# Attention and two MoE layers on one core: a head's cast in two halves, zeros moved to the start of GpSimd, a unit's input copied on chip

## The chip, the cores and the metric

One Trainium2 chip, one of its cores. The metric is the device time of one execution in microseconds (us), as a median of several runs. The engines are TensorE (PE in the profile, with PEld for its weight loads), VectorE (DVE), ScalarE (ACT), GpSimd (POOL) and SyncE (SP, which here only issues DMAs).

## What is computed

The input is `q`, `k`, `v` of 4 batches with 8 heads of 576 rows and 64 columns, a decay factor `f`, and the weights of two feed-forward layers. Everything is float32.

```python
scores = scale * q @ k.T
cum = cumsum(log(clip(f, 0.0001, 1.0)))
scores = where(causal, -1e9, scores + cum[:, None] - cum[None, :])
attn = exp(scores - max(scores)); attn = attn / (sum(attn) + 1e-09)
x = (attn @ v)                    # to 2304 tokens x 512
x = square(max(x @ w_in, 0)) @ w_out          # 512 -> 2048 -> 512
x = elu(x @ w2_in) @ w2_out                   # 512 -> 2048 -> 512
```

## The kernel before, in words

**Precision.** A float32 product is made of three fp32r products of rounded operands: high by high, low by high, high by low. So each operand is first cast to its rounded value and then subtracted from the original for the low part. The cast is `copy` (L125; its VectorE form is L131), the subtraction is `minus` (L119), which on GpSimd is L136.

**Order of the work.** Attention runs in steps, written out in the list `todo`; a head pair has five of them: parts A of both heads, a joint part "4", parts B of both. In each step `soft` (L635) makes the scores and the exponentials, and `outs` (L645) one step later (`LAG`) turns and splits them and multiplies by `v`. Between the pieces, `fill` (L890) puts matmuls of the first feed-forward layer for the first six units of 256 tokens (`unit`, L723). A scheduler with a time line then sets the order in which each engine's queue stands, and the few `tc.issue_after(...)` in the code bind it.

**Scores and row maxima.** A tile of scores is written by TensorE (`scores`, L436; for a rounded head two matmuls per block, L442 and L443), read by VectorE (`reduce_min`, L446, which leaves the negated row maximum in `nm` by an accumulator read), and turned into exponentials by ScalarE (`expo`, L448). The scores have two buffers: the third tile can begin only when VectorE has reduced the first. That is the place where TensorE can wait for VectorE ("s L442 <- DVE nm L446").

**The heads.** Batch 0 is done in plain F32 ("Plain", no cast). The 24 heads of batches 1 to 3 are "rounded" heads of part "F". `load_head` (L398) prepares one, two steps ahead (`AHEAD`): the raw tile of 128x1280 (704 columns for q, 576 for k) is cast to `qk1` by **one VectorE instruction** (L131), four rows of decay go by DMA to `qk2` (L424), GpSimd makes q's low part (64x704, L136), a DMA moves k's rounded part from `qk1` to `qk2` (L427), GpSimd makes k's low part (64x576, L136) and splits v (L129 and L136). `qk1`, `raw` and `qk2` have three buffers each.

**Outputs.** `out_a`, `out_b` and `fold` (L522) gather a head pair's x in 64x256 or 64x320 pieces on VectorE, `split_pt` (L508, lines L509 and L510) splits a turned tile, `norm_x` (L535) scales with one over the row sums, and `store_x` (L547) splits x into `xs` (ScalarE high, L553; low by L123 or L136) and stores it to `x1` in DRAM (L556). `load_x1` (L697) loads a unit's input back as `xu` (L701). The input of unit 0 stays on chip as `x0`.

**Opening.** `block_zeros` (L264) clears, behind a copy named `quiet`, two strips of the tiles of part "4" (`e4s`), a mask `m4` and half an identity, all on GpSimd; it first waits for the cumulated decay.

Of the kernel before, what the change touches and what calls it, by code (L numbers as in the profile page):

```python
# [19 lines left out]
NC = DM // 128  # L20
# [15 lines left out]
PACE = (1.28, 0.9, 1.85, 1.75)  # L36
COST = {'A': 0.7, '4': 1.1, 'B': 1.7}
W_AT = (1, 1, 1, 1, 0, 0, 0, 0, 2, 2, 2, 2, 2, 2)
AHEAD = 2
FETCH = 4  # L40
LAG = 1
# [42 lines left out]
def attention_then_moe_kernel(ctx, tc, first, firstv, plain, qkv, f, w1, w2, out):  # L84
# [125 lines left out]

    fr = ab.tile([32, S], F32, tag="eb", name="fr", bufs=BUFS["eb"])
    nc.sync.dma_start(out=fr, in_=f)
    x0 = xa.tile([128, 2 * NC, CH], F32R, tag="xu", name="x0")
    raws_w = xa.tile([128, 2, 512, 2], I32, tag="xu", name="raws_w")
    mz = a1.tile([128, 512], F32, name="mz")
    m4 = a1.tile([128, 288], F32, name="m4")
    ptA = [[a1.tile([128, 512], F32R, name=f"ptA{s}{t}") for t in range(2)] for s in range(2)]
# [3 lines left out]
    ca = wa.tile([B * H, 4, 512], F32R, tag="w7", name="ca")  # L221
    me.memset(f32(ca[:, 0:2, 256:512]), 1.0)
    me.memset(f32(ca[:, 2:4, 0:256]), 1.0)
    nc.gpsimd.memset(mz, 0.0)
    mask(mz[:, 384:512], [[-1, 128]])

# [37 lines left out]
    def block_zeros():  # L264
        quiet = nc.gpsimd.tensor_copy(go, f32(made[1][:, 1, S - 257:S - 256]))
        with tc.issue_after(quiet.ins):
            for s in range(2):
                nc.gpsimd.memset(e4s[s][:, S:640], 0.0)
            nc.gpsimd.memset(m4, 0.0)
            nc.gpsimd.tensor_copy(ident[:, 128:192], ident[:, 0:64])  # L270
            for k in range(2):
                mask(m4[64 * k:64 * k + 64, 224:288], [[-1, 64]])
# [125 lines left out]
    def load_head(b, h, part):  # L398
        q0, q1, k1, js = {"F": (0, QW, S, 5), "A": (Q0, QW, 256, 2), "B": (0, Q0, S, 5)}[part]
        w = "ABF".index(part)  # L400
        raw = raws.pop((b, h, part))
        if isinstance(raw, Plain):
            return raw
        raw, rv = raw
        vr = rv[:, 0:js * D].rearrange("p (j d) -> p j d", d=D)
        qk1 = hd.tile([128, RAW], F32R, tag="qk1", name="qk1", bufs=BUFS["qs"])
        qk2 = a1.tile([128, RAW], F32R, tag="qk2", name="qk2", bufs=3)
        kc = slice(QW, QW + k1)
        qc = slice(q0, q1)
        g = b * H + h  # L410
        if part == "A":
            ac = slice(Q0, QW + 256)
            copy(ENG["qk"][w], qk1[:, ac], raw[:, ac])
        else:
            ac = slice(0, RAW)
            if part == "F":
                copy(ENG["qk"][w], qk1, raw[:, ac])
            else:
                copy(ENG["qk"][w], qk1[:, qc], raw[:, qc])
                copy(ENG["qk"][w], qk1[:, kc], raw[:, kc])  # L420
        if part == "A":
            nc.sync.dma_start(out=f32(qk2[64:68, ac]), in_=f32(ca[g:g + 1]))
        else:
            nc.sync.dma_start(out=f32(qk2[64:68, ac]), in_=aug[g - H, :, ac])  # L424
        minus(ENG["ql"][w], qk2[0:64, qc], raw[0:64, qc], qk1[0:64, qc])
        if ENG["kh"][w] == "d":
            nc.sync.dma_start(out=f32(qk2[0:64, kc]), in_=f32(qk1[0:64, kc]))  # L427
        else:
            copy(ENG["kh"][w], qk2[0:64, kc], f32(qk1[0:64, kc]))
        minus(ENG["kl"][w], qk1[64:128, kc], raw[64:128, kc], qk1[64:128, kc])  # L430
        vv = hd.tile([128, 5, 2 * D], F32R, tag="vv", name="vv", bufs=BUFS["vv"])
        copy(ENG["vh"][w], vv[:, 0:js, 0:D], vr)
        minus(ENG["vl"][w], vv[:, 0:js, D:2 * D], vr, vv[:, 0:js, 0:D])
        return qk1, qk2, vv
# [112 lines left out]
    def store_x(b, hp, x, c0, n):  # L547
        if b in SPLIT and c0 == 0:
            xs = x0[:, hp::NC]
        else:  # L550
            xs = a1.tile([128, 2, 320], F32R, tag="xs", name="xs", bufs=BUFS["xh"])
        c = slice(0, n)
        nc.scalar.activation(out=xs[:, 0, c], in_=x[:, c], func=AF.Copy)  # L553
        minus(ENG["xl"][b > 0], xs[:, 1, c], x[:, c], xs[:, 0, c])
        if not (b in SPLIT and c0 == 0):
            nc.sync.dma_start(out=x1[b][hp::NC, :, c0:c0 + n].rearrange("c p t -> p c t"), in_=f32(xs[:, :, c]))  # L556

    def out_a(hh, e, x, k):
        pt = ps_t.tile([128, 512], F32, tag="t", name="pt")
# [68 lines left out]
    e4 = {}  # L628
    es = {}
    xs = {}  # L630

    def load(b, hp, k, part):
        heads[b, hp, k] = load_head(b, 2 * hp + k, part)

    def soft(b, hp, kind, k):  # L635
        if kind == "A":
# [58 lines left out]
        return gh, gl  # L695

    def load_x1(t0, n, pool):  # L697
        x = pool.tile([128, 2 * NC, n], F32R, tag="xu", name="xu")
        for c in range(NC):
            for off, step, b, s in runs(t0, n):  # L700
                nc.sync.dma_start(out=f32(x[:, c::NC, off:off + step]), in_=x1[b][c::NC, :, s:s + step].rearrange("c p t -> p c t"))  # L701
        return x
# [145 lines left out]
        return False  # L848

    credit = 0.0  # L850
    for i in range(len(todo) + LAG):
        at_step[0] = i
        if i == 0:
# [11 lines left out]
                aug_rows(True)  # L865
        while fetches and fetches[0][0] <= i + FETCH and i > max(BEGIN):
            fetch_head(*fetches.pop(0)[1:])
        while loads and loads[0][0] <= i + AHEAD:
            load(*loads.pop(0)[1:])
        if i < len(todo):  # L870
            sg = soft(*todo[i])
# [18 lines left out]
        def fill():  # L890
# [14 lines left out]
            if not started[0] and not went and i < FILL_TO:  # L905
                with tc.issue_after(seen[0].ins):
                    busy(FILL + (step == 1))

        drain(sg)
        fill()  # L910
        for _ in og:
            fill()
# [384 lines left out]
```

## Time and profile before

| what | us |
|---|---|
| median of 3 runs | 1026.14 (1025.92 to 1027.38) |
| the profiled execution itself | 1025.79 |
| span in that profile, first to last instruction | 1024.0 |
| PE busy | 1011.2 (99%) |
| DVE busy | 709.2 (69%) |
| ACT busy | 522.9 (51%) |
| POOL busy | 257.3 (25%) |

The first 345 us hold the attention with the first units of the first layer; after that come feed-forward layers alone. The instructions of GpSimd lie almost all in the first 345 us, so that its 25% are more like three quarters there. TensorE's granted clock is 1.00 in nearly all of the span.

### The profile page before, as it was taken

How to read it: one execution, taken by the hardware profiler on the slowest of the kernel's cores; microseconds unless marked ns; L12 is line 12 of the kernel's file. 1: busy time of each engine (PE TensorE's matmuls, PEld its weight loads, DVE VectorE, ACT ScalarE, POOL GpSimd, SP SyncE). 2: the span in 40 equal slices, each digit the busy share in tenths (PEclk: the TensorE clock that was granted, in tenths of full speed). 3: DMA queues.
4: the chain of work that ended last, by engine and by line, in shares of the span. 5: the costliest groups of instructions: out<-in, count | busy, mean ns of one | idle time of the engine just before them, and what ended most of it. 6: DMA issues, size and time to landing. Idle time of an engine off the chain costs nothing.

```text
span 1024.0 us, 17635 instructions
## 1 busy us (share of the span) xinstructions
PE 1011.2 (99%) x6363; PEld 899.2 (88%) x6363; DVE 709.2 (69%) x1595; ACT 522.9 (51%) x1196; POOL 257.3 (25%) x282
## 2 busy tenths in 40 slices
PE   9999999999999999999999999999999999999998
PEld 8777799899999988889988888998889988899997
DVE  8894788766775548845376779895455989654554
ACT  7674676766676634423243445553334555333331
POOL 2135697675774300012104040400000000000000
PEclk9999999999999999999999999999999999999999
DMA  8847547454531074443545645653415556353402
GB/s 212 271 140 208 171 137 227 146 153 124 183 106 62 24 259 125 143 132 116 175 139 211 210 169 197 234 178 113 145 42 185 165 186 207 102 182 126 147 21 83
DMA packets 77334, 157.59 MB, mean 154 GB/s; under 512 B 9616, under 2 KB 38032, under 8 KB 77248
## 3 DMA queue, kind: packets, MB, share of 16 engines
q1 hardware_dynamic: 77232, 156.46, 47.5%
q8 instruction: 50, 0.82, 0.3%
q14 instruction: 36, 0.29, 0.1%
q10 hardware_dynamic: 16, 0.02, 0.0%
HBM read 113.94 MB, written 38.90 MB: 149 GB/s over the span
## 4 chain that ended last, share of the span: by engine, by line
PE 95%; DVE 2%; DMA 1%; ACT 1%; POOL 1%; issue 0%; ACTq 0%; POOLq 0%; SPq 0%
PE O L192 33%; PE P L192 18%; PE pH L192 13%; PE ph L192 7%; PE o L192 6%; PE pt L513 5%; PE pv L520 4%; PE s L438 3%; PE pv L517 2%; PE s L442 2%; PE s L443 2%; PE idle L289 1%; DMA xu<-x 1%; PE pr L513 1%; DVE qk L131 0%
## 5 line engine op out<-in xcount | busy, mean ns | idle before, releaser
L192 PEld LDWEIGHTS P<-xu,v 128*128 128x128 f32 x1536 | 200.1, 189 | 10.8 <-issue 0.5
L192 PE MATMUL P<-xu,v 128*128 128x256 f32 x1536 | 203.7, 282 | 0.7 <-DMA xu<-x 0.7
L192 PE MATMUL O<-v,gh 128*128 128x512 f32 x576 | 171.1, 393 | 0.0
L192 PE MATMUL pH<-xu,w 128*128 128x512 f32 (+1 forms) x672 | 140.8, 360 | 0.0
L192 PEld LDWEIGHTS pH<-xu,w 128*128 128x128 f32 x672 | 114.0, 188 | 20.2
L192 PE MATMUL O<-gh,w 128*128 128x512 f32 (+1 forms) x448 | 122.6, 362 | 0.0
L192 PEld LDWEIGHTS O<-v,gh 128*128 128x128 f32 x576 | 102.8, 188 | 17.6
L1142 ACT ACTIVATE hs<-P 128x256 f32<-128x256 f32 x128 | 48.4, 381 | 113.8 <-PE P L192 113.0
L192 PE MATMUL O<-v,gl 128*128 128x512 f32 x288 | 103.5, 393 | 0.0
L192 PEld LDWEIGHTS O<-gh,w 128*128 128x128 f32 x448 | 79.8, 189 | 14.1
L136 POOL TENSOR_TENSOR yl<-pr,yh 128x512 fp32r<-128x512 f32 x18 | 25.1, 1394 | 248.5 <-ACT yh L962 174.7
L1145 DVE TENSOR_TENSOR hs<-P,hs 128x256 f32<-128x256 f32 x96 | 40.5, 422 | 62.2 <-PE P L192 58.9
L136 POOL TENSOR_TENSOR qk<-raw,qk 64x704 fp32r<-64x704 f32 (+1 forms) x48 | 77.1, 1606 | 17.6 <-DVE qk L131 5.2
L192 PE MATMUL O<-gl,w 128*128 128x512 f32 (+1 forms) x224 | 80.1, 363 | 0.0
L192 PE MATMUL o<-gh,w 128*128 128x256 f32 x384 | 76.1, 292 | 0.0
L157 ACT ACTIVATE wt<-wraw 128x512 f32<-128x512 f32 x57 | 38.4, 673 | 58.5 <-DMA wraw<-in_w_dram 39.4
L192 PE MATMUL ph<-xu,w 128*128 128x256 f32 x480 | 66.8, 287 | 0.3 <-DMA xu<-x 0.3
L682 ACT ACTIVATE gh<-g 128x512 fp32r<-128x512 f32 (+1 forms) x80 | 46.9, 586 | 38.2 <-DVE g L681 34.9
L681 DVE TENSOR_TENSOR g<-g 128x512 f32<-128x512 f32 (+1 forms) x56 | 45.1, 805 | 28.3 <-ACT g L677 28.1
L192 PEld LDWEIGHTS O<-v,gl 128*128 128x128 f32 x288 | 53.1, 188 | 10.3
L1113 ACT ACTIVATE gh<-g 128x512 fp32r<-128x512 f32 x72 | 45.4, 631 | 32.3 <-DVE g L1168 25.4
L192 PEld LDWEIGHTS o<-gh,w 128*128 128x128 f32 x384 | 60.3, 191 | 1.4 <-issue 0.5
(166 smaller groups left out, 2045.5 us busy)
## 6 DMA issues: line engine op xcount, KB each, us to landing
xu<-x SPq DMA_DIRECT2D x66, 512.0 KB
wraw<-in_w_dram SPq DMA_DIRECT2D x57, 512.0 KB
raw<-in_qkv_dram SPq DMA_DIRECT2D x24, 640.0 KB
x<-yh SPq DMA_DIRECT2D x31, 256.0 KB
x<-yl SPq DMA_DIRECT2D x31, 256.0 KB
x<-xs SPq DMA_DIRECT2D x16, 320.0 KB
xu<-x SPq DMA_DIRECT2D x16, 256.0 KB
rv<-in_qkv_dram SPq DMA_DIRECT2D x24, 160.0 KB
```

Of the source, the lines that this page charges most:

```text
L136: nc.gpsimd.tensor_tensor(out=dst, in0=x, in1=f32(hi), op=ALU.subtract)
L157: nc.scalar.activation(out=f32(t), in_=f32(hi), func=AF.Abs)
L192: nc.tensor.matmul(out=dst, lhsT=l, rhs=r, start=first and i == 0, stop=last and i == n - 1, skip_group_check=skip)
L438: seen[0] = nc.tensor.matmul(out=dst, lhsT=hh.t[0:68, hh.q + q0:hh.q + q0 + 128], rhs=hh.t[0:68, hh.k + j0:hh.k + j0 + n], start=first, st ...
L442: nc.tensor.matmul(out=dst, lhsT=qk1[:, q0:q0 + 128], rhs=qk1[:, QW + j0:QW + j0 + n], start=first, stop=False)
L513: seen[0] = nc.tensor.transpose(dst, src, ident[:, c0:c0 + 128])
L520: seen[0] = nc.tensor.matmul(out=dst, lhsT=hh[2][:, J, :], rhs=hl[i], start=first and i == 0, stop=last and i == 1)
L681: (nc.vector if sq == "v" else nc.gpsimd).tensor_tensor(out=g[:, 0:n], in0=g[:, 0:n], in1=g[:, 0:n], op=ALU.mult)
L682: nc.scalar.activation(out=gh[:, 0:n], in_=g[:, 0:n], func=AF.Copy)
L1113: nc.scalar.activation(out=gh, in_=g, func=AF.Copy)
L1142: nc.scalar.activation(out=o, in_=x, func=AF.Copy)
L1145: nc.vector.tensor_tensor(o, y, x, op=ALU.add)
```

## The change

Three edits:

- **Cast in two halves.** `load_head` for a rounded head becomes a generator `whole_head`. Its first half casts q's 704 columns, issues the decay rows and q's low part; it is bound behind the last row maximum of the step in which it is asked for (`reduced[-1]`), and heads are asked for one step earlier (`AHEAD + 1`). In the next step the second half casts k's 576 columns behind the first row maximum of that step, and then issues the DMA of k's rounded part, k's low part and v's split.
- **Zeros.** The two strips of `e4s` are cleared among the first instructions of GpSimd, ahead of the mask `mz`, and no longer in `block_zeros`.
- **Unit 1's input.** Its tile `second` is allocated at step 14 (`OPEN`). When `store_x` has stored the second part of batch 0's x for head pairs 1 to 3, a further DMA copies the first 256 columns from `xs` to that tile on chip, and `load_x1` leaves those three loads out. The store to `x1` stays. The tiles `raws_w` and `x0` of the same pool swap their order of declaration.

```diff
+    for s in range(2):
+        nc.gpsimd.memset(e4s[s][:, S:640], 0.0)
     nc.gpsimd.memset(mz, 0.0)
...
         with tc.issue_after(quiet.ins):
-            for s in range(2):
-                nc.gpsimd.memset(e4s[s][:, S:640], 0.0)
             nc.gpsimd.memset(m4, 0.0)
...
-                copy(ENG["qk"][w], qk1, raw[:, ac])
...
+        with tc.issue_after(behind[0].ins):
+            copy(ENG["qk"][w], qk1[:, qc], raw[:, qc])
...
         minus(ENG["ql"][w], qk2[0:64, qc], raw[0:64, qc], qk1[0:64, qc])
+        yield
+        with tc.issue_after(behind[0].ins):
+            copy(ENG["qk"][w], qk1[:, kc], raw[:, kc])
         if ENG["kh"][w] == "d":
             nc.sync.dma_start(out=f32(qk2[0:64, kc]), in_=f32(qk1[0:64, kc]))
...
             nc.sync.dma_start(out=x1[b][hp::NC, :, c0:c0 + n].rearrange("c p t -> p c t"), in_=f32(xs[:, :, c]))
+            if not b and second:
+                nc.sync.dma_start(out=f32(second[0][:, hp::NC, :]), in_=f32(xs[:, :, 0:CH]))
+                here.add(hp)
...
-        x = pool.tile([128, 2 * NC, n], F32R, tag="xu", name="xu")
+        x = second[0] if t0 == CH else pool.tile([128, 2 * NC, n], F32R, tag="xu", name="xu")
         for c in range(NC):
+            if t0 == CH and c in here:
+                continue
...
-        while loads and loads[0][0] <= i + AHEAD:
+        while loads and loads[0][0] <= i + AHEAD + (loads[0][4] == "F"):
             load(*loads.pop(0)[1:])
...
+        n_red = len(reduced)
         drain(sg)
+        for h in coming:
+            behind[0] = reduced[min(n_red, len(reduced) - 1)]
+            second_half(*h)
+        if i == OPEN:
+            second.append(xa.tile([128, 2 * NC, CH], F32R, tag="xu", name="xu"))
+        coming = halves_[:]
+        halves_.clear()
+        for h in coming:
+            behind[0] = reduced[-1]
+            first_half(*h)
         fill()
```

How the order moves is seen on VectorE in the fourth head pair of batch 1. `ISA eb.., nm..` is a row maximum (its second row reads the accumulator), CAST the cast of a head, `p`, `ptB` the split of a turned tile, `xs`, `xB`, `xA` pieces of the output. Before:

```order
L446 ISA eb_2736,nm2_2737<-s_2739,mz_126 128x512
L446 ISA nm2_2737 128x1
L131 CAST qk1_2762<-raw_2663 128x1280
L446 ISA eb_2736,nm2_2737<-s_2744,mz_126 128x384
L446 ISA nm2_2737 128x1
L510 TENSOR_TENSOR ptB01_133<-pt_2513,ptB00_132 128x256
L123 TENSOR_TENSOR xs_2418<-xA_2344,xs_2418 128x256
L510 TENSOR_TENSOR p1_2557<-pt_2552,p0_2556 128x320
L446 ISA eb_2772,nm2_2773<-s_2774,mz_126 128x512
L446 ISA nm2_2773 128x1
```

Now (the line numbers have moved by two):

```order
L448 ISA eb_2741,nm2_2742<-s_2744,mz_126 128x512
L448 ISA nm2_2742 128x1
L132 CAST qk1_2697<-raw_2631 128x576
L454 TENSOR_SCALAR z1_2678<-z1_2678 128x1
L448 ISA eb_2741,nm2_2742<-s_2749,mz_126 128x384
L448 ISA nm2_2742 128x1
L132 CAST qk1_2760<-raw_2673 128x704
L512 TENSOR_TENSOR p1_2567<-pt_2562,p0_2566 128x320
L512 TENSOR_TENSOR p1_2575<-pt_2570,p0_2574 128x320
L531 TENSOR_TENSOR xB_2493<-pv_2510,t_2547 64x320
L448 ISA eb_2778,nm2_2779<-s_2780,mz_126 128x512
L448 ISA nm2_2779 128x1
```

Between the row maxima of 512 and 384 columns, which free the two score buffers, a whole cast of one head stood; now the k half of one head stands there, and a q half of another behind the second row maximum.

The second place is SP's queue at the end of batch 0, where the last pieces of unit 1's input are issued (`x1_0` and `x1_1` are batch 0 and 1 in DRAM; `xu_1469` and `xu_1041` are the tile of unit 1, `xu_2717` and `xu_2732` that of the unit after it). Before:

```order
L556 DMA x1_0_71<-xs_1435 128x2x320
L427 DMA qk2_1830<-qk1_1829 64x576
L306 DMA rv_2034<-in_qkv_dram 128x320
L701 DMA xu_1469<-x1_0_71 128x2x256
L701 DMA xu_2717<-x1_0_71 128x2x64
```

Now:

```order
L558 DMA x1_0_71<-xs_1440 128x2x320
L560 DMA xu_1041<-xs_1440 128x2x256
L307 DMA rv_2040<-in_qkv_dram 128x320
L724 DMA xu_2732<-x1_0_71 128x2x64
```

The last load of unit 1's tile from DRAM is gone; a copy from `xs` stands right behind the store.

## Rows read from the trace of the kernel before

**Rows 1.** The page: busy time of each engine, share of the span, instructions.

```profile
PE 1011.2 (99%) x6363; PEld 899.2 (88%) x6363; DVE 709.2 (69%) x1595; ACT 522.9 (51%) x1196; POOL 257.3 (25%) x282
```

**Rows 2.** The page: the chain that ended last, by engine.

```profile
PE 95%; DVE 2%; DMA 1%; ACT 1%; POOL 1%; issue 0%; ACTq 0%; POOLq 0%; SPq 0%
```

**Rows 3.** Waits of TensorE: total us, times, longest us.

```profile
PE s L442 <- DVE nm L446: 3.5, 4, 1.3
PE s L438 <- DVE wt L161: 1.7, 1, 1.7
...
PE pt L513 <- DVE p L510: 0.8, 1, 0.8
...
PE ph L192 <- DMA xu<-x: 0.3, 1, 0.3
```

**Rows 4.** Windows: us, then busy of PE, PEld, DVE, ACT, POOL; clock, DMA, GB/s.

```profile
25.00:50.00 25.00, 22.76 (x122) 17.32 (x121) 21.51 (x57) 17.38 (x44) 4.69 (x16) 0.93 0.93 279
120.00:145.00 25.00, 24.08 (x191) 23.37 (x189) 19.95 (x64) 19.32 (x55) 20.59 (x21) 1.00 0.60 193
145.00:170.00 25.00, 22.89 (x176) 21.36 (x174) 23.16 (x64) 19.53 (x54) 22.45 (x23) 1.00 0.57 160
170.00:200.00 30.00, 28.41 (x225) 27.13 (x224) 23.03 (x74) 20.45 (x58) 17.57 (x23) 1.00 0.61 196
200.00:345.00 145.00, 145.00 (x1178) 143.41 (x1177) 100.83 (x290) 98.88 (x262) 91.57 (x102) 1.00 0.38 116
```

**Rows 5.** Time line of TensorE: start us, us, instruction, [idle before <- releaser].

```profile
121.19 0.35 PE L442 MATMUL s<-qk 128*128 128x256 f32 x1 [0.63 <-DVE nm L446]
168.08 0.36 PE L442 MATMUL s<-qk 128*128 128x256 f32 x1 [1.27 <-DVE nm L446]
...
170.00 0.40 PE L192 MATMUL o<-gh,w 128*128 128x256 f32 x2
...
170.36 0.40 PE L192 MATMUL o<-gh,w 128*128 128x256 f32 x2
...
170.72 0.38 PE L513 MATMUL pt<-ident,e 128*128 128x128 f32 x2
170.94 0.27 PE L513 MATMUL pt<-ident,eb 128*128 128x128 f32 x1
```

**Rows 6.** Time line of VectorE around two of these waits.

```profile
119.02 1.54 DVE L131 CAST qk<-raw 128x1280 fp32r<-128x1280 f32 x1
120.49 0.55 DVE L446 CUSTOM_DVE_ANT_0 eb<-s,mz 128x384 f32<-128x384 f32 x1
...
165.73 1.73 DVE L131 CAST qk<-raw 128x1280 fp32r<-128x1280 f32 x1
...
168.19 1.38 DVE L123 TENSOR_TENSOR xs<-xA,xs 128x256 fp32r<-128x256 f32 x1
```

**Rows 7.** Time line of GpSimd at the same two places.

```profile
119.01 0.87 POOL L136 TENSOR_TENSOR xs<-xB,xs 128x320 fp32r<-128x320 f32 x1
...
163.58 3.20 POOL L136 TENSOR_TENSOR qk<-raw,qk 64x704 fp32r<-64x704 f32 x2 [0.82 <-issue]
```

**Rows 8.** All instructions of VectorE on the tile qk: ns min/median/max.

```profile
L131 DVE CAST qk<-raw x24: 808/828/1729, 76.9 to 314.7; 128x1280 fp32r<-128x1280 f32 x24
```

**Rows 9.** VectorE from 100 to 345 us by shape: busy us, mean ns.

```profile
L510 DVE TENSOR_TENSOR p<-pt,p 128x320 fp32r<-128x320 f32 x68 | 31.9, 483 | 10.4 <-ACT p L509 9.9
L131 DVE CAST qk<-raw 128x1280 fp32r<-128x1280 f32 x22 | 22.4, 1020 | 3.6 <-PE s L442 3.5
L446 DVE CUSTOM_DVE_ANT_0 eb<-s,mz 128x512 f32<-128x512 f32 x25 | 17.1, 684 | 3.6 <-PE s L443 2.7 <-PE s L438 0.6
L446 DVE CUSTOM_DVE_ANT_0 eb<-s,mz 128x384 f32<-128x384 f32 x25 | 13.7, 548 | 0.2 <-PE s L443 0.2
...
L510 DVE TENSOR_TENSOR ptB<-pt,ptB 128x256 fp32r<-128x256 f32 x22 | 9.1, 414 | 2.8 <-ACT ptB L509 2.7
```

**Rows 10.** Time line of GpSimd in the opening.

```profile
9.57 0.22 POOL L268 MEMSET e<- 128x64 f32 x2
```

More of the change, by code (lines that the diff above doesn't have):

```diff
@@ L38 @@
 W_AT = (1, 1, 1, 1, 0, 0, 0, 0, 2, 2, 2, 2, 2, 2)
+OPEN = 14
 AHEAD = 2
@@ L212, in attention_then_moe_kernel @@
     nc.sync.dma_start(out=fr, in_=f)
+    raws_w = xa.tile([128, 2, 512, 2], I32, tag="xu", name="raws_w")
     x0 = xa.tile([128, 2 * NC, CH], F32R, tag="xu", name="x0")
-    raws_w = xa.tile([128, 2, 512, 2], I32, tag="xu", name="raws_w")
     mz = a1.tile([128, 512], F32, name="mz")
@@ L403, in load_head, with whole_head @@
             return raw
+        return whole_head(b, h, part, raw, q0, q1, k1, js, w)
+    behind = [None]
+    def whole_head(b, h, part, raw, q0, q1, k1, js, w):
         raw, rv = raw
@@ L410, in load_head @@
         g = b * H + h
[L411 to L416, printed above, removed]
-                copy(ENG["qk"][w], qk1, raw[:, ac])
-            else:
-                copy(ENG["qk"][w], qk1[:, qc], raw[:, qc])
-                copy(ENG["qk"][w], qk1[:, kc], raw[:, kc])
+        ac = slice(Q0, QW + 256) if part == "A" else slice(0, RAW)
+        with tc.issue_after(behind[0].ins):
+            copy(ENG["qk"][w], qk1[:, qc], raw[:, qc])
         if part == "A":
@@ L630, in attention_then_moe_kernel, with first_half, second_half @@
     xs = {}
+    second, here = [], set()
     def load(b, hp, k, part):
-        heads[b, hp, k] = load_head(b, 2 * hp + k, part)
+        head = load_head(b, 2 * hp + k, part)
+        if isinstance(head, Plain):
+            heads[b, hp, k] = head
+        else:
+            halves_.append((head, (b, hp, k)))
+    halves_ = []
+    def first_half(head, key):
+        next(head)
+    def second_half(head, key):
+        try:
+            next(head)
+        except StopIteration as e:
+            heads[key] = e.value
     def soft(b, hp, kind, k):
@@ L850, in attention_then_moe_kernel @@
     credit = 0.0
+    coming = []
     for i in range(len(todo) + LAG):
```

## The prediction

> **What bounds the kernel now.** I read the page first: TensorE is busy for 99% of the span [rows 1] and holds 95% of the chain that ended last [rows 2]. So only what lets TensorE wait, or takes a wait away, can move the time, and there is little to take away: its table of waits [rows 3] shows 3.5 us in four waits for row maxima of VectorE, 0.8 us for a split of VectorE, 0.3 us for unit 1's input and 1.7 us in the opening. The windows [rows 4] say where. From 120 to 200 us, TensorE is busy for 24.08 + 22.89 + 28.41 of 80 us: 4.6 us are missing, nearly the sum of the first three (3.5 + 0.8 + 0.3). From 200 to 345 us, with 16 of the 24 rounded heads still to go, nothing is missing: 145.00 of 145.00. After 345 us no head is left. So the change is decided in batch 1, in some 80 us.
>
> Two of the waits stand at 121.19 and 168.08 us on TensorE's time line [rows 5]. What held VectorE is a row away [rows 6]: at 119.02 a cast of 1.54 us stands ahead of the row maximum that frees the scores' buffer, and at 165.73 one of 1.73 us. Over all 24 the shortest is 0.808, the median 0.828, the longest 1.729 us [rows 8]; the mean from 100 us on is 1.020 [rows 9]. The long ones are not longer in work. GpSimd was within an instruction when they began [rows 7]: one ended at 119.88 and the cast at 120.56, one pair ended at 166.78 and the cast at 167.46, each 0.68 us later. A cast, it seems, can't do its work until the GpSimd instruction in flight is over. The output piece at 168.19, 1.38 us for 256 columns [rows 6], is of the same sort, since a turned tile of 256 columns is split in 0.414 [rows 9].
>
> **The cast in two halves.** Number: 24 casts go, 24 of 704 and 24 of 576 columns come, beside otherwise the same instructions. Price of an unblocked half: splits of 320 and 256 columns take 0.483 and 0.414 us [rows 9], 1.08 ns for a column and 0.137 us for an instruction. The cast's 0.828 less 0.137 is 0.54 ns a column, so that the halves take 0.52 and 0.45. On a busy VectorE an instruction begins some 0.08 us before the one ahead has ended (119.02 + 1.54 is 120.56, the next begins at 120.49 [rows 6]), so in a row they cost 0.44 and 0.37 where the whole cost 0.75: 0.06 us more a head, 1.4 us on VectorE in all, most of it beside TensorE's work.
>
> What matters is where they stand. In the new order each head pair of batch 1 has one stretch in which four halves (of two heads) come between row maxima that free TensorE's score buffers, with the splits and output pieces of the pair. I priced VectorE's rows there by [rows 9] less 0.08 each (row maxima 0.60 for 512 and 0.47 for 384 columns, splits 0.40 for 320 and 0.33 for 256; other sizes by 1.08 ns a column). TensorE's pace is three matmuls of 256 columns in 0.36 us, from 170.00 to 170.36, so 0.47 ns a column, and two transposes in 0.22 us from 170.72 [rows 5], 0.11 each.
>
> - Fourth pair (the one shown in the order): VectorE has row maxima 0.37 + 2 x 0.60 + 2 x 0.47, four halves 1.61, splits 4 x 0.40 + 2 x 0.33, pieces 0.33 + 0.40, two small ones 0.12, together 7.2 us; TensorE has 9,344 columns, 4.4, and 17 transposes, 1.9, together 6.3. VectorE is late by 1.0.
> - Third pair: five large row maxima and two small ones 3.0, halves 1.6, splits 0.9, pieces and small ones 2.3, in all 7.9; TensorE 13,760 columns and 11 transposes, 7.7. Late by 0.2.
> - First pair: 7.7 against 10,176 columns and 20 transposes, 7.0. Late by 0.7.
> - Second pair: even.
>
> That sums to **1.9 us of waits even when no half is blocked**. To it comes what the halves lose to GpSimd, which in 120 to 170 us is busy for 43.0 of 50 us [rows 4]. Whole casts lost 1.020 - 0.828 = 0.2 us on the mean. For a half I have no row. Below, it loses nothing (none begins within an instruction of GpSimd); above, as much as the whole casts of the two waits shown, 0.72 (1.54 - 0.82) and 0.91 (1.73 - 0.82). I take the whole's mean, 0.2, since halves are anchored behind row maxima, at times that have no relation to GpSimd's: 16 halves, 3.2 us. An output piece caught as the one at 168.19 costs 1.0; I take half of one, 0.5. Sum of the new waits 1.9 + 3.2 + 0.5 = 5.6, in place of 3.5 + 0.8 = 4.3: **+1.3 us**. In batches 2 and 3 the extra 0.06 a head lies beside TensorE, for VectorE is busy for only 100.8 of 145 us there [rows 4]: nothing, at most 1 us if one stretch there ran out of cover.
>
> The Trainium skill has a rule that speaks against this change ("SBUF — State Buffer", Terms, shared port pair): VectorE and GpSimd share a pair of ports, which one of them holds for a full instruction while the other fully blocks. By the rule alone, worked out from this trace's rows, a half would find GpSimd within an instruction 86 times in 100 and wait for half of one of 1.6 us, 0.69 on the mean: 11.0 us for 16 halves in place of 3.2, and a time of 1034.9. The trace agrees that a cast can be held (the two ends 0.68 us after GpSimd's [rows 6, 7]), but not with that mean: whole casts lost 0.2.
>
> The rest of a head's steps keep their number (decay rows, q's low part, k's copy, k's low part, v's split). On SP's queue, k's copy stands behind the second half, later than before by a step at most, but heads are asked for a step earlier. It has cover as long as a head is ready before its first scores (third rival).
>
> **Unit 1's input.** Three loads from DRAM become copies on chip behind the stores. The wait of 0.3 us goes [rows 3]; it may come back in part, since the last copy still stands behind the last `xs`. I take -0.3, with 0 and -0.3 as ends. The tile `xs` has one buffer and is now read by two DMAs; its next writer comes a step later, and that hides it: 0. The store no longer has to land before SP's next entries go on, which helps SP's queue by nothing on the path.
>
> **Zeros.** Two instructions begin from 9.57 us, 0.22 us for the later one and the overlap [rows 10], and move to a time when GpSimd waits for nothing. TensorE's opening wait of 1.7 us [rows 3] is put down to a weight split on VectorE, and its operand comes by a DMA; neither is touched. Between 0 and -0.2; I take 0.
>
> **Sum.** +1.3 - 0.3 = +1.0 on the profiled execution's 1025.8: 1026.8. The median lies 0.35 above it, so that the **predicted time is 1027.1 us**. What a measurement can tell from no change is about 0.2%, 2.05 us: below 1024.1 is faster, above 1028.2 slower.
>
> **Rivals.**
>
> 1. *The halves fall into free gaps (faster).* For it: the two longest waits each had a whole cast ahead of a row maximum [rows 5, 6], and a half there is shorter by 0.3 us; short instructions have a smaller chance to be in anyone's way. Then only the 1.9 us remain where 4.3 were, with the 0.3 of the input: -2.7 us, **1023.4**. Against it: GpSimd's 86% from 120 to 170 us.
> 2. *The k half runs into its own head's low part (slower).* The q half releases GpSimd's q part, one of a pair of 3.20 us, so 1.6 us long [rows 7]. If the k half comes behind the first row maximum of the next step while that or the next subtraction is in flight, it pays as the cast at 119.02 did, 0.72, in each of four stretches, twice; q halves 0.2. Waits: 1.9 + 0.5 + 8 x 0.72 + 8 x 0.2 = 9.8, less 4.3 and 0.3: +5.2, **1031.3**. It decides from a mean loss of 0.33 us for a k half: there 8 x (0.33 + 0.2) + 2.4 - 4.6 is 2.0, the edge of slower. A single long wait could also cost clock: in the window of the 1.7 us wait, 25 to 50 us, the granted clock was 0.93 [rows 4], and 7% of 25 us are 1.7 us. Against that: after the 1.27 us at 168.08, the window shows 1.00.
> 3. *A head is ready too late.* The change casts k later. By the new order and TensorE's pace, three heads have 3.8 to 4.3 us of matmuls from the k half to their first scores. The half itself, a GpSimd instruction in flight and k's low part are 0.45 + 1.6 + 1.6 = 3.7; with one more of GpSimd's ahead, TensorE waits up to 1.6 at each. At 0.7 for each of three: +2.1, with the +1.0 above **1029.2**.
> 4. *The change doesn't do what it says.* Zeros and input are that case already: if neither wait goes, the sum is +1.3 and not +1.0, within the forecast.
>
> **How the numbers follow.** The forecast holds from 1024.1 to 1028.2, mean losses of a half between nearly 0 and 0.33 us: 0.42. The first rival 0.22. The second 0.24 (of it 0.02 for the blocking at each half, 1034.9, which whole casts do not bear out) and the third 0.12, both slower. So faster 0.22, same 0.42, slower 0.36. The range reaches from 1022.9, half a us under the first rival, to 1030.9, just short of the second rival's whole price, past the third; the forecast's own is 1025.0 to 1028.2.
>
> **What would show it.** In the changed profile there should be 24 casts of 704 and 24 of 576 columns, the short ones near 0.52 and 0.45 us, and long ones ending a fixed time after a GpSimd instruction. If the second rival is right, the mean of the k halves is above 0.8 us and TensorE's waits for row maxima sum to over 6 us, spread over the four head pairs of batch 1, the first at about 100 us, where none is now. If the first is right, both means lie within 0.1 us of the short ones and the waits sum to under 2.5. The third would show as waits of the scores' weight load or matmul for a DMA or for GpSimd. The wait for unit 1's input should be gone, and the opening's 1.7 us and its clock should be as they were. The forecast is wrong if any wait of more than 0.5 us comes from 200 us on, or if the opening changes.

## The result: slower by 0.8%

The changed kernel takes **1034.6 us** (median of 6 runs, 1033.96 to 1040.04) beside 1027.14 of the kernel before on the same chip: a ratio of 1.0081, 95% interval [1.0057, 1.0106]. The forecast was 1027.1, the range 1022.9 to 1030.9; the time lies above it, and on the side of slower.

The page of the changed kernel, to be read beside [rows 1] and [rows 2]; the second line is the granted clock in 40 slices of 25.8 us, the third the chain.

```profile
PE 1015.0 (98%) x6363; PEld 901.0 (87%) x6363; DVE 722.8 (70%) x1619; ACT 523.6 (51%) x1196; POOL 257.1 (25%) x282
...
PEclk9999999899999999999999999999999999999999
...
PE 82%; DVE 8%; DMA 4%; ACT 2%; issue 2%; POOL 2%; SPq 1%; POOLq 0%; ACTq 0%; DVEq 0%
```

VectorE is busy for 13.6 us more (722.8 for 709.2; part of that is waiting for GpSimd, as shown below) and has 8% of the chain where it had 2%. The span is 1032.8, 8.8 longer. Where it went is in the windows (columns as in [rows 4]).

```profile
25.00:50.00 25.00, 23.86 (x132) 17.35 (x133) 23.25 (x60) 18.57 (x46) 4.76 (x15) 1.00 0.87 265
...
100.00:125.00 25.00, 23.36 (x155) 18.35 (x154) 16.43 (x53) 15.77 (x46) 13.38 (x16) 1.00 0.60 186
125.00:150.00 25.00, 22.60 (x176) 21.46 (x175) 20.60 (x55) 17.28 (x46) 19.68 (x21) 1.00 0.38 116
150.00:175.00 25.00, 21.99 (x155) 20.30 (x155) 20.39 (x57) 15.61 (x46) 15.86 (x18) 0.93 0.51 159
175.00:200.00 25.00, 22.33 (x153) 21.08 (x152) 22.40 (x62) 15.75 (x46) 18.04 (x21) 0.86 0.59 177
...
300.00:350.00 50.00, 49.28 (x397) 48.29 (x396) 35.16 (x102) 33.48 (x90) 28.69 (x32) 1.00 0.19 63
```

From 100 to 200 us TensorE misses 1.64 + 2.40 + 3.01 + 2.67 = 9.7 us; before it missed 4.6 in that stretch. The clock is 0.93 and 0.86 in the last two windows: 7% and 14% of 25 us, 5.2 us. From 300 to 350 us 0.7 are missing, where before nothing was. The opening gives 2.5 back (its window has clock 1.00 where [rows 4] has 0.93, and 0.7 us less idle in the first 50 us). So +5.1 + 5.2 + 0.7 - 2.5 = 8.5 of the 8.8 us.

TensorE's waits show a line that the kernel before had not at all, beside those that answer to [rows 3]:

```profile
PE pv L522 <- DVE xA L531: 4.3, 5, 1.8
PE s L444 <- DVE nm L448: 1.9, 3, 1.2
PE pt L515 <- DVE p L512: 1.6, 2, 1.3
...
PE pv L522 <- DVE xB L531: 0.9, 1, 0.9
...
PE s L440 <- DVE wt L161: 0.6, 1, 0.6
...
PE ph L193 <- DMA xu<-xs: 0.4, 1, 0.4
```

The row maxima, which the prediction looked at, cost less than before (1.9 for 3.5). The new wait is that of a product with v (`av`) for VectorE to fold the one before (`xA`, `xB`, L531). And the wait for unit 1's input has not gone: 0.4 where it was 0.3.

Four of the waits on TensorE's time line of the changed kernel:

```profile
142.53 0.74 PE L522 MATMUL pv<-ptA,vv 128*128 128x256 f32 x4 [1.80 <-DVE xA L531]
...
161.48 0.74 PE L522 MATMUL pv<-ptA,vv 128*128 128x256 f32 x4 [1.15 <-DVE xA L531]
...
191.10 0.50 PE L444 MATMUL s<-qk 128*128 128x512 f32 x1 [1.22 <-DVE nm L448]
...
193.90 0.66 PE L515 MATMUL pt<-ident,e 128*128 128x128 f32 x2 [1.28 <-DVE p L512]
```

What VectorE did ahead of these four:

```profile
138.42 3.25 DVE L124 TENSOR_TENSOR xs<-xB,xs 128x320 fp32r<-128x320 f32 x1
...
159.38 1.72 DVE L132 CAST qk<-raw 128x576 fp32r<-128x576 f32 x1
...
188.58 1.86 DVE L124 TENSOR_TENSOR xs<-xA,xs 128x256 fp32r<-128x256 f32 x1
...
191.88 1.48 DVE L132 CAST qk<-raw 128x704 fp32r<-128x704 f32 x1
```

And GpSimd at the first three:

```profile
138.09 1.99 POOL L137 TENSOR_TENSOR qk<-raw,qk 64x704 fp32r<-64x704 f32 x1
140.04 1.28 POOL L137 TENSOR_TENSOR gl<-g,gh 128x512 fp32r<-128x512 f32 x1
...
159.10 1.68 POOL L137 TENSOR_TENSOR qk<-raw,qk 64x704 fp32r<-64x704 f32 x1
...
188.01 1.73 POOL L137 TENSOR_TENSOR qk<-raw,qk 64x704 fp32r<-64x704 f32 x1 [1.20 <-DVE qk L132]
189.70 0.46 POOL L130 TENSOR_SCALAR vv<-rv 128x320 fp32r<-128x320 f32 x1
```

The k half at 159.38 ends at 161.10, 0.32 us after the subtraction at 159.10 (its end is 160.78). The two output pieces, which read two tiles, wait for two each, the one in flight and the next: that at 138.42 ends at 141.67, 0.35 after the instruction that began at 140.04 has ended; that at 188.58 ends at 190.44, 0.28 after the 0.46 at 189.70. GpSimd went on from one instruction to the next and VectorE stayed out, for 3.25 us in place of some 0.47. (An expectation below counts three instructions for the first piece; the rows show two, since the one before had ended when the piece began.)

In this profile the clock fell twice, each time behind several waits close together. Windows of 2 us around the first fall (columns as in [rows 4]):

```profile
160.00:162.00 2.00, 0.85 (x7) 0.64 (x6) 2.00 (x4) 0.31 (x2) 1.54 (x2) 1.00 0.06 13
162.00:164.00 2.00, 1.57 (x9) 1.17 (x8) 1.90 (x9) 1.65 (x5) 1.30 (x2) 0.55 0.74 208
164.00:166.00 2.00, 2.00 (x11) 1.98 (x12) 1.30 (x5) 1.61 (x7) 0.28 (x1) 0.59 0.96 319
```

After 160 to 162, where TensorE was busy for 0.85 of 2 us, the clock stands near half (1.2 of 2.4 GHz); the two windows lack 0.45 and 0.41 of 2 us, so that it was at half for 3.4 us. The single wait of 1.80 us at 142.53 brought no fall here. That is not a rule. In a second profile of the same kernel (the whole change again, below) TensorE has a wait of 1.79 us at 144.86 in that wait's place, and there the clock fell behind it, while the run of waits some 20 us later cost no clock:

```profile
146.00:148.00 2.00, 1.78 (x8) 1.34 (x7) 1.53 (x6) 1.98 (x9) 0.60 (x2) 0.50 0.94 321
...
162.00:166.00 4.00, 2.30 (x17) 1.73 (x15) 4.00 (x11) 1.67 (x5) 3.54 (x3) 1.00 0.16 40
```

From 100 to 200 us the clock is 0.95 in both profiles. So the waits and what they cost in clock come again; which of them is followed by a fall does not.

### The profile page after: what moved, and what is told of

It reads as the page before. It is cut to its first block, busy times and chain, and to the rows that moved or that the text cites. A ratio compares the mean times of both kernels' runs of the same rounds, so it can differ in the third digit from the quotient of the medians.

```text
span 1032.8 us, 17676 instructions
## 1 busy us (share of the span) xinstructions
PE 1015.0 (98%) x6363; PEld 901.0 (87%) x6363; DVE 722.8 (70%) x1619; ACT 523.6 (51%) x1196; POOL 257.1 (25%) x282
## 4 chain that ended last, share of the span: by engine, by line
PE 82%; DVE 8%; DMA 4%; ACT 2%; issue 2%; POOL 2%; SPq 1%; POOLq 0%; ACTq 0%; DVEq 0%
PE O L193 29%; PE P L193 15%; PE pH L193 11%; PE ph L193 6%; PE o L193 6%; PE pt L515 5%; PE pv L522 4%; PE pv L519 2%; PE s L445 2%; PE s L444 2%; PE s L440 1%; DMA x<-yl 1%; DVE qk L132 1%; DMA wraw<-in_w_dram 1%; DMA aug<-ok 1%
## 5 line engine op out<-in xcount | busy, mean ns | idle before, releaser
L193 PEld LDWEIGHTS P<-xu,v 128*128 128x128 f32 x1536 | 200.1, 189 | 11.0 <-DMA xu<-x 0.7
L193 PE MATMUL P<-xu,v 128*128 128x256 f32 x1536 | 203.8, 282 | 0.9 <-DMA xu<-x 0.8
L193 PE MATMUL O<-v,gh 128*128 128x512 f32 x576 | 171.1, 393 | 0.0
L193 PE MATMUL pH<-xu,w 128*128 128x512 f32 (+1 forms) x672 | 140.8, 360 | 0.0
L193 PEld LDWEIGHTS pH<-xu,w 128*128 128x128 f32 x672 | 114.0, 188 | 20.2
L193 PE MATMUL O<-gh,w 128*128 128x512 f32 (+1 forms) x448 | 122.6, 362 | 0.0
L193 PEld LDWEIGHTS O<-v,gh 128*128 128x128 f32 x576 | 102.8, 188 | 17.6
L193 PE MATMUL O<-v,gl 128*128 128x512 f32 x288 | 103.5, 393 | 0.0
L193 PEld LDWEIGHTS O<-gh,w 128*128 128x128 f32 x448 | 79.8, 189 | 14.1
L193 PE MATMUL O<-gl,w 128*128 128x512 f32 (+1 forms) x224 | 80.1, 363 | 0.0
L193 PE MATMUL o<-gh,w 128*128 128x256 f32 x384 | 77.1, 293 | 0.0
L193 PE MATMUL ph<-xu,w 128*128 128x256 f32 x480 | 69.4, 289 | 0.6 <-DMA xu<-xs 0.4
L193 PEld LDWEIGHTS ph<-xu,w 128*128 128x128 f32 x480 | 61.6, 191 | 1.2 <-DMA xu<-xs 0.7
L193 PEld LDWEIGHTS O<-v,gl 128*128 128x128 f32 x288 | 53.1, 188 | 10.3
```

The source lines that it names most:

```text
L193: nc.tensor.matmul(out=dst, lhsT=l, rhs=r, start=first and i == 0, stop=last and i == n - 1, skip_group_check=skip)
```

## The experiments

### The parts alone and in pairs

Theory A: the halves make the loss. Rivals: the copied input, or the zeros, or the parts together. Three runs hold one part each, and one the zeros and the input with whole casts.

```diff
# e1_zeros, e15_zeros_again: the kernel before, with
+    for s in range(2):
+        nc.gpsimd.memset(e4s[s][:, S:640], 0.0)
     nc.gpsimd.memset(mz, 0.0)
# e2_halves: the change without its lines on zeros, second, raws_w
# e3_input, e4_zeros_input: the change with
-            copy(ENG["qk"][w], qk1[:, qc], raw[:, qc])
+        copy(ENG["qk"][w], qk1, raw[:, ac])
...
# and heads asked for two steps ahead again; in e3_input the zeros stand where they stood before
```

> Only the two zeroings of the strips move to the start of GpSimd. In the changed profile the opening ends some 2.9 us earlier (the same turned matmul of batch 0 at 94.11 instead of 97.04 us). Theory A, the zeros make that gain (they no longer stand ahead of the mask on GpSimd): about 1023.5 us, with the wait of 1.7 us before the scores of rawC shorter and no fall of the clock in 25 to 50 us. Rival, the gain comes from the order of declaration or from where transfers happen to land: 1026 to 1027, as before.

> Only the cast in two halves (asked for one step earlier); zeros and unit 1's input as before. Theory: the halves alone make the whole loss, since VectorE's half casts and output pieces stand behind GpSimd instructions in flight and TensorE waits for it in batch 1, and the clock falls after the waits: 1035 to 1038 us, TensorE missing 8 to 10 us between 100 and 200 us, and clock under 0.95 in two windows of 25 us there. Rival, the halves cost little and the loss comes from the copied input or from an order of the queues that only the three together give: under 1029.

> Only unit 1's input copied on chip, with the swapped declaration of raws_w and x0; whole casts and zeros as before. Theory: the wait of 0.3 us for that input goes and nothing else: 1025.5 to 1026.5. Rival: the swapped declaration makes the opening's gain: 1023 to 1024. Second rival: the copies hold SP's queue or the one xs buffer and cost: 1027 and more.

> The change with whole casts: zeros and input as in the change, a head's cast in one instruction, asked for two steps ahead as before. Theory: without the halves the loss is gone and the opening's gain stays: 1023 to 1024.5, faster than both. Rival, the loss isn't the halves': 1030 or more.

| run | median us | ratio to before | 95% interval |
|---|---|---|---|
| zeros | 1025.6 | 0.9970 | [0.9951, 0.9989] |
| halves | 1029.0 | 0.9996 | [0.9980, 1.0011] |
| input | 1026.6 | 0.9991 | [0.9976, 1.0006] |
| zeros and input, whole casts | 1028.0 | 0.9998 | [0.9982, 1.0015] |

Theory A fell: the halves alone cost nothing that can be measured. Nor does the input or the zeros. So it takes two of them together, or all three. (Each ratio is to the kernel before on the chip of that run, where its median lay between 1026.6 and 1028.7; medians of different tables don't compare.)

> Halves and zeros, unit 1's input as before. The zeros change no engine's order behind the opening, so the order of batch 1 is that of the halves alone. Theory B (the loss needs the order that halves and copied input give together): 1026 to 1030 us, within 0.3% of before, 4 to 5 us missing on TensorE from 100 to 200 us. Rival (halves alone were lucky, any disturbance of the opening makes the loss): 1033 or more.

> Halves and copied input, zeros as before. On every engine but GpSimd's opening the order is that of the whole change. Theory B: the whole loss is here, 1033 to 1037 us, with 9 to 10 us missing on TensorE from 100 to 200 us and a clock under 0.95 there in at least one window of 25 us. Rival (the three parts together, or the opening's earlier end): under 1030.

> The whole change once more, beside the others on the same chip. Theory B: 1033 to 1037 us, a ratio of 1.006 to 1.010 to before; the output piece of 3.25 us and the two falls of the clock come again at the same instructions. Rival (they were an accident of one chip): under 1030.

| run | median us | ratio to before | 95% interval |
|---|---|---|---|
| halves and zeros | 1028.0 | 1.0016 | [0.9997, 1.0035] |
| halves and input | 1035.1 | 1.0083 | [1.0058, 1.0108] |
| the whole change again | 1035.5 | 1.0088 | [1.0064, 1.0112] |

The whole loss is in halves and input together, and theory B (the loss needs the order that halves and input give together) holds. In the two runs of that table that have both, the output piece of 3.25 us comes again (3.25 and 3.24). The zeros add nothing here, and their gain alone didn't come again: the same kernel with more rounds gave 1027.3, a ratio of 0.9997 [0.9977, 1.0016].

> The zeros alone once more, with more rounds. Alone they gave a ratio of 0.997, but beside halves, input or both they gave 1.0005 to 1.002 (from the medians). If the gain is real: 0.996 to 0.998 again. If not: an interval that holds 1.

### The halves' holds

Over all 24 heads the halves alone lose as much time to GpSimd as those of the change. VectorE by shape from 75 to 345 us (busy us, mean ns), in the change:

```profile
L132 DVE CAST qk<-raw 128x576 fp32r<-128x576 f32 x24 | 22.2, 927 | 0.0
L132 DVE CAST qk<-raw 128x704 fp32r<-128x704 f32 x24 | 18.4, 766 | 0.0
```

and with the halves alone:

```profile
L132 DVE CAST qk<-raw 128x576 fp32r<-128x576 f32 x24 | 25.7, 1070 | 0.0
L132 DVE CAST qk<-raw 128x704 fp32r<-128x704 f32 x24 | 16.2, 675 | 0.0
```

That is 25.7 + 16.2 = 41.9 us, against 22.2 + 18.4 = 40.6 with the whole loss. But that is not so in the stretch that decides. From 100 to 200 us, in the change:

```profile
L132 DVE CAST qk<-raw 128x576 fp32r<-128x576 f32 x11 | 11.0, 1003 | 0.0
L132 DVE CAST qk<-raw 128x704 fp32r<-128x704 f32 x10 | 8.6, 857 | 0.0
```

and with the halves alone:

```profile
L132 DVE CAST qk<-raw 128x576 fp32r<-128x576 f32 x11 | 10.0, 906 | 0.0
L132 DVE CAST qk<-raw 128x704 fp32r<-128x704 f32 x10 | 6.5, 652 | 0.0
```

There the halves alone lose 3 us less. So these lines don't clear the holds: the order of the change has more of them in batch 1. What speaks against them as the whole cause comes with the runs on the cover below.

At one place the halves alone have an output piece held nearly as long as the one of the change, at no cost. Halves alone, VectorE's time line:

```profile
202.84 3.02 DVE L124 TENSOR_TENSOR xs<-xA,xs 128x256 fp32r<-128x256 f32 x1
```

That stretch as a window of the halves alone: TensorE's busy time is all of it.

```profile
202.80:205.90 3.10, 3.10 (x28) 3.10 (x27) 3.10 (x3) 1.21 (x4) 2.77 (x2) 1.00 0.00 0
```

The same window for the matmuls of the feed-forward layer alone (line L193; busy of PE and PEld, then clock and DMA):

```profile
202.80:205.90 3.10, 2.51 (x19) 2.15 (x18) 1.00 0.00 0
```

In the change, around its piece of 3.25 us, the window of all engines:

```profile
138.40:141.70 3.30, 2.17 (x16) 1.96 (x16) 3.30 (x3) 1.97 (x6) 3.30 (x3) 1.00 0.25 55
```

and of line L193 alone:

```profile
138.40:141.70 3.30, 1.69 (x12) 1.49 (x12) 1.00 0.25 55
```

With 19 feed-forward matmuls TensorE is full while VectorE is held; with 12 it stands still for 1.1 us of that stretch and more behind it. Five runs were to ease the holds.

```diff
# e8_cast_act: the change with the half casts of rounded heads on ScalarE
-ENG = {'qk': 'aav', ...
+ENG = {'qk': 'aaa', ...
# e12_k_act: the change with the k halves alone there
-            copy(ENG["qk"][w], qk1[:, kc], raw[:, kc])
+            copy("a", qk1[:, kc], raw[:, kc])
# e9_xs_pool: the change with the low part of xs on GpSimd
-... 'xl': 'pv'}
+... 'xl': 'pp'}
# e10_adjacent: the change with the k half in the q half's step
-        yield
         with tc.issue_after(behind[0].ins):
             copy(ENG["qk"][w], qk1[:, kc], raw[:, kc])
+        yield
# e11_zeros_act: zeros alone, whole casts on ScalarE ('qk': 'aaa')
```

> The whole change, but the half casts of rounded heads run on ScalarE instead of VectorE. Theory A (VectorE loses its time to GpSimd's instructions in flight at the halves): 19 us of casts leave VectorE, TensorE misses under 5 us from 100 to 200 us, 1022 to 1028 us. Rival (the halves' places and the heads' readiness cost, whichever engine casts; or ScalarE becomes late): 1032 or more.

> The whole change, but the low part of the output pieces xs of batches 1 to 3 is made by GpSimd and not by VectorE. In the change one such piece took 3.25 us on VectorE, behind three GpSimd instructions in a row. Theory A1 (the blocked output pieces carry the loss): the longest wait for xA is gone, TensorE misses under 7 us from 100 to 200 us, under 1031 us. Theory A2 (the half casts carry it, and a busier GpSimd blocks them more): 1033 us or more.

> The whole change, but the k half is cast in the same step as the q half, behind the same row maximum; the rest of the head comes a step later as in the change. Theory (each half can be blocked wherever it stands, and it is the later k halves that are): the k half's mean comes down from 0.96 towards 0.6 us since GpSimd hasn't begun the head's low part yet, and the time to 1027 to 1031. Rival (two instructions in place of one cost as such, or the step of lead does): 1033 or more.

> Before with the zeros moved and the whole casts of rounded heads on ScalarE; no halves, no copied input. Theory A (VectorE's waits in batch 1 are casts and pieces held by GpSimd): of the 3.5 us of waits for row maxima at least 2 go, 1022 to 1025 us, and faster than before and than the zeros alone. Rival (ScalarE's exponentials then come late): 1026 or more.

> The whole change, but the k halves alone run on ScalarE. By the second rival of the prediction (the k half behind its own head's low part carries the loss): 1027 to 1030 us, as TensorE gets back 6 us of blocked VectorE time. If q halves and output pieces carry it as much: 1032 or more.

| run | median us | ratio to before | 95% interval |
|---|---|---|---|
| half casts on ScalarE | 1026.4 | 0.9987 | [0.9970, 1.0003] |
| low part of xs on GpSimd | 1030.4 | 1.0022 | [1.0002, 1.0042] |
| k half in the same step | 1029.1 | 1.0010 | [0.9987, 1.0032] |
| zeros, whole casts on ScalarE | 1027.3 | 1.0014 | [0.9991, 1.0036] |
| k halves on ScalarE | 1029.2 | 1.0012 | [0.9990, 1.0035] |

The four that hold the whole change took most of the loss away, the one that made the k halves *longer* too: with the pieces on GpSimd they are 1.30 us on the mean, in place of 0.93, and the ratio is 1.0022 where the change has 1.0081. On ScalarE a half takes 0.66 to 0.81 us, with no long ones, and still nothing is won against before; nor by whole casts there, although these cut the waits for row maxima from 3.5 to 0.5 us. By their numbers, three of these four fall where the theory that blames the hold had put them (half casts on ScalarE, k half in the same step, k halves on ScalarE); with the pieces on GpSimd the time does too, but TensorE misses 7.2 us from 100 to 200 where under 7 was expected. But each of these edits also gave TensorE another order, so none of them alone tells hold from order.

Two did. They change only the form of the half cast, and every instruction stands where it stood in the change.

```diff
# e13_scalar_form
-            copy(ENG["qk"][w], qk1[:, qc], raw[:, qc])
+            nc.vector.tensor_scalar(qk1[:, qc], raw[:, qc], 1.0, 0.0, op0=ALU.mult, op1=ALU.add)
# e14_strided (in both, the k half likewise)
+            nc.vector.tensor_copy(qk1[:, qc].rearrange("p (n t) -> p t n", t=2),
+                                  raw[:, qc].rearrange("p (n t) -> p t n", t=2))
```

> The whole change with the half casts written as a multiplication by one (TENSOR_SCALAR) in place of a copy. Every engine's instructions stand in the order of the change, one for one, so nothing but this instruction differs. If TENSOR_SCALAR meets GpSimd as the copy does, all stays: halves of 0.52 and 0.45 us when free, means near 0.80 and 0.96, 1033 to 1037 us. If it is one that GpSimd doesn't hold, the spread between shortest and longest half goes (all within 0.2 us) and the time comes down to 1030 or less.

> The whole change with the half casts reading and writing every second column, twice (2x352 and 2x288 in place of 704 and 576). The order is that of the change on all engines, one for one. Theory A (the loss is VectorE held by GpSimd in flight, at the places which this order gives): a slower form that GpSimd doesn't hold takes 0.7 to 0.9 us each time, with no long ones, the means as in the change or lower; the output pieces are still held. If what costs is being held at the wrong moment, the longest waits shrink and the time is 1028 to 1032; if VectorE's total is what counts, or the order alone, it stays at 1033 to 1037.

Both missed as tests of the hold: neither form is slower or escapes it (means of 0.77 us for q and 0.94 to 0.95 for k). They gave 1036.3 (ratio 1.0087 [1.0067, 1.0106]) and 1036.4 (1.0101 [1.0077, 1.0124]). What they show is that the order brings the same waits back. TensorE with the strided form:

```profile
144.78 0.74 PE L522 MATMUL pv<-ptA,vv 128*128 128x256 f32 x4 [1.79 <-DVE xA L531]
...
164.71 0.73 PE L522 MATMUL pv<-ptA,vv 128*128 128x256 f32 x4 [1.15 <-DVE xA L531]
```

1.79 and 1.15 us, as 1.80 and 1.15 in the change. No kernel was found that keeps the order and takes the hold away, so that experiment wasn't made.

### The cover

Theory C: with unit 1's input declared ready earlier, feed-forward matmuls stand earlier in TensorE's order, and are used up where the holds come. Those matmuls alone (line L193), in stretches of 10 us of the change:

```profile
120.00:130.00 10.00, 4.90 (x34) 4.38 (x34) 1.00 0.57 171
...
186.00:196.00 10.00, 0.00 (x0) 0.00 (x0) 0.85 0.51 151
```

Before (line L192):

```profile
120.00:130.00 10.00, 2.06 (x15) 1.85 (x15) 1.00 0.77 251
...
186.00:196.00 10.00, 3.31 (x24) 3.07 (x24) 1.00 0.64 196
```

34 in place of 15 from 120 to 130 us (with the halves alone 26), and from 186 to 196, where the waits of 1.22 and 1.28 us and the second fall of the clock are, none in place of 24 (with the halves alone 24). Two runs warn against reading these counts alone. The input alone has 39 from 120 to 130 us and loses nothing. And the halves alone, which lose nothing either, have hardly any from 180 to 190:

```profile
180.00:190.00 10.00, 0.54 (x4) 0.35 (x4) 1.00 0.50 141
```

So a stretch without cover is not enough; a hold has to fall into it. Three runs keep all of the change and only shift these matmuls.

```diff
# e16_unit_later
-DELAY = 0
+DELAY = 1
# e17_pace_08; e18_pace_07 has 0.7
-PACE = (1.28, 0.9, 1.85, 1.75)
+PACE = (1.28, 0.8, 1.85, 1.75)
```

> The whole change with each first-layer unit begun one chance later (a delay of 1 in place of 0). Theory C (the copied input lets the feed-forward matmuls of unit 1 and 2 run ahead, so that none are left to cover VectorE where GpSimd holds it: in the change TensorE has no such matmul from 186 to 196 us): the holds of halves and pieces stay (mean of k halves still over 0.85 us, q over 0.6), but matmuls of the feed-forward layer stand in every stretch of 10 us from 100 to 200, TensorE misses 6 us or less there, no clock under 0.95 after 100 us, 1027 to 1030 us. Rival (the holds alone): 1033 or more.

> The whole change with the pace of feed-forward steps in batch 1 at 0.8 in place of 0.9. Theory C: the cover is spread further, so as in the run with the delay: 1027 to 1031 us with the holds much as they are. Rival: 1033 or more.

> The whole change with that pace at 0.7. Theory C: 1026 to 1030 us; by it, less feed-forward work is done in batch 1 and the rest moves to a time when TensorE is full anyway. Rival: 1033 or more.

| run | median us | ratio to before | 95% interval | mean of k and q halves, us |
|---|---|---|---|---|
| unit one chance later | 1032.5 | 1.0059 | [1.0040, 1.0078] | 1.05, 0.80 |
| pace 0.8 | 1050.1 | 1.0227 | [1.0207, 1.0247] | 0.96, 0.80 |
| pace 0.7 | 1030.1 | 1.0032 | [1.0016, 1.0047] | 1.02, 0.72 |

The first missed its numbers, the second lies far on the side of its rival, and the third is at the upper end of its range. Theory C said that spreading wins; it didn't say that a pace of 0.8 would spread, and it doesn't. The feed-forward matmuls of that run:

```profile
160.00:170.00 10.00, 0.00 (x0) 0.00 (x0) 0.95 0.48 144
...
180.00:190.00 10.00, 0.71 (x5) 0.57 (x4) 0.80 0.46 127
```

Two stretches with next to no cover, and the clock at 0.95 and 0.80 there. They are only part of that run's loss: its span is 22.7 us longer than before, and from 200 to 345 us alone TensorE misses 7.3 us (before: none) and the clock falls twice more, once behind a single wait of 1.66 us for k's copy at 290.39. I don't know what made the waits after 200 us. At a pace of 0.7 the poorest stretch from 120 us on has 1.96:

```profile
150.00:160.00 10.00, 1.96 (x15) 1.57 (x13) 1.00 0.62 183
```

and TensorE misses 5.8 us from 100 to 200, with the clock at 1.00.

Here is what VectorE lost to GpSimd from 100 to 200 us, beside what TensorE missed there. A loss is the time of the half casts (or of the output pieces `xs`) less their number times the shortest of their shape from 75 to 345 us: in the change 11 x (1.003 - 0.448) + 10 x (0.857 - 0.521) = 9.5.

| run | casts lost, us | pieces lost, us | TensorE misses, us | clock | ratio to before |
|---|---|---|---|---|---|
| before (whole casts) | 2.7 | 4.8 | 4.6 | 1.00 | 1 |
| halves alone | 6.5 | 3.0 | 4.5 | 1.00 | 0.9996 |
| the change | 9.5 | 5.2 | 9.7 | 0.95 | 1.0081 |
| unit one chance later | 9.3 | 0.8 | 7.0 | 0.98 | 1.0059 |
| pace 0.8 | 8.6 | 1.9 | 7.9 | 0.95 | 1.0227 |
| pace 0.7 | 9.7 | 1.3 | 5.8 | 1.00 | 1.0032 |

The two paces lose as much to GpSimd (10.5 and 11.0 us) and differ by 2.1 us of waits and 0.05 of clock in this stretch, and by 20 us in time. So the sum of the holds does not set the loss. The pace adds and removes no instruction; what differs between these two runs is the order, and with it where the holds fall. Against the change, a pace of 0.7 is no such test, for its halves are held as long but its pieces 3.9 us less. That is what these runs show. They don't show that cover is the whole of it, nor how the loss of the change divides between less cover and more hold: the run with the delay has 23 or more such matmuls in every stretch from 150 to 200 and still loses 0.6%. Its largest waits are others (1.6 us for unit 1's input, 1.6 for ScalarE's copy of a piece), and I can't say which of them the delay itself brought.

## Why the prediction was wrong

**What held.** TensorE bounds the kernel, and batch 1 decides. A free half takes 0.52 and 0.45 us: the shortest are 0.521 and 0.448. From 200 to 345 us next to nothing is lost (0.7 us, the bound was 1), though it comes as one wait of 0.7 us at 328.69, for a GpSimd subtraction, and any wait of over 0.5 us there was named as a sign of being wrong; so was a changed opening, and the opening's wait is 0.6 where it was 1.7. The zeros are worth nothing. VectorE is held while a GpSimd instruction is in flight.

**The step that failed first: "Unit 1's input. [...] I take -0.3".** I priced three DMAs and a wait, and added that to the halves' price as if neither could change the other. But when the input of a unit is ready sets where the scheduler puts its matmuls, and with them the order of what follows. Beside whole casts the input costs nothing (0.9991); beside halves it costs 7 to 9 us (1035.1 against 1028.0 with halves and zeros on one chip; 1.0083 against 0.9996 for the halves alone). What in that order costs them is not shown to the end: from 100 to 200 us the change has both more hold than the halves alone (14.7 us against 9.5) and no cover where the last holds come, and no run took one away and kept the other. The -0.3 itself didn't come either: the wait is 0.4 us.

**Second: the stretches.** I took four, each up to the row maxima that free the score buffers, and compared sums of VectorE's and TensorE's work. The longest waits came elsewhere, at the products with v, which wait for VectorE to fold the last product: 5.2 of the 8.7 us in the first four lines of waits above that name VectorE's work in batch 1. A sum over a stretch also hides where the cover lies in it: at 138.42 TensorE had 12 feed-forward matmuls, ran out of them and stood still for 1.80 us.

**Third, three sizes.** The mean loss of a half was put at 0.2 us, as of whole casts. From 100 to 200 us it was 0.56 for k (1.003 - 0.448) and 0.34 for q (0.857 - 0.521), 0.45 together: 9.5 us for 21 halves, where the sum has 3.2 for 16. Over all 24 heads it was 0.48 and 0.25, 0.36 together. An output piece was priced at 1.0 when held, by one instruction; one was held through two, 2.8 us more than when free. All pieces together lost hardly more than before (5.2 for 4.8 us); only their places changed. The clock was priced at 0 in the sum: it cost 5.2 us in the profile, as much as the new waits.

**The rivals.** The second (1031.3, plus 1.7 for a fall of the clock: 1033.0) came near in time and named the k half behind its own head's low part; the trace shows just that at 159.38, and the mean of the k halves is above 0.8 us, as it asked. But its other sign did not come: the waits for row maxima sum to 1.9 us, not to over 6. And as a whole cause it falls with the halves alone: from 100 to 200 us k halves there take 0.91 us, 0.46 more than a free one, above the 0.33 from which it was to decide, at a ratio of 0.9996. The Trainium skill's rule ("SBUF — State Buffer", Terms, shared port pair), by which I worked out 1034.9 and to which I gave 0.02, is nearer the truth in one thing than my mean: the loser fully blocks, and the piece of 3.25 us shows it block through the rest of one instruction and the whole of the next. Its mean of 0.69 us a half doesn't come; 0.45, from 100 to 200 us, lies about half way between it and my 0.2. That the time agrees with 1034.9 is luck, since 5.2 us of it are clock, which that sum had at 0, and the halves alone, which GpSimd holds too, lose nothing. The third rival, a head ready too late, isn't in the changed profile; with the halves alone, three waits for k's copy sum to 2.0 us.

## What to carry to other kernels

Where an engine at 98% waits only in a short stretch, look in the new order at what covers it at the places of the holds, window by window, and do so for every edit that changes when some work becomes ready, however small its own cost. Two edits that are each neutral can be slow together, so try the pairs. And idle time on TensorE can cost twice: in the change 5.1 us of new waits brought 5.2 us of clock with them, while at a pace of 0.7 TensorE missed 5.8 us there at no cost in clock.

## What the runs showed beside that

- An instruction of VectorE with two operands in SBUF can be kept out through more than one GpSimd instruction: 3.25 us for 320 columns and 3.02 for 256, each behind two. A cast can be too: with the pieces on GpSimd the longest k half took 2.93 us. A cast and its strided or multiplying forms are held alike; the splits and folds, which read PSUM, took their usual time beside the same GpSimd work (0.41 us for the fold at 142.07, as at other times; all 66 splits of 320 columns in the change from 75 to 345 us lie between 0.46 and 0.49).
- The waits for DMAs differ between executions of one and the same kernel. The zeros alone, first profile and second:

```profile
PE s L438 <- DMA rawC<-augb: 0.8, 1, 0.8
PE ph L192 <- DMA xu<-x: 0.5, 1, 0.5
```

```profile
PE ph L192 <- DMA xu<-x: 2.4, 1, 2.4
PE s L438 <- DMA rawC<-augb: 1.7, 1, 1.7
```

That is 2.8 us between two profiles, so the 2.5 us that the opening gave back in the changed profile prove nothing for the change, and one look doesn't rank kernels that lie within 0.3%.
